# A recurrent attention with two expert layers on one core: later copies of the inverses, two sets of inversion buffers, one subtract on VectorE, and another order of the beginning

## The chip, the cores and the metric

The kernel runs on one core of a Trainium2 chip. The metric is device time in microseconds (us) of one execution. The engines are named as the profile does: PE is TensorE (its weight loads are PEld), DVE is VectorE, ACT is ScalarE, POOL is GpSimd, SP is SyncE. A row with SPq or ACTq is the issue of a DMA by SyncE's or ScalarE's queue.

## What is computed

The inputs are 4 batches of 8 heads with 768 steps of width 40, and the weights of two token layers. Cut to what matters:

```python
for t in range(S):                       # 768 steps, state 40x40 per head
    y[:, :, t] = einsum('bhd,bhde->bhe', rt, state)
    Sa = einsum('bhde,bhe->bhd', state, at)
    state = state * wt - Sa x bt + vt x kt          # outer products
x = y as 3072 tokens of width 320
x = ((x @ w_a) * (x @ w_b)) @ w_out                 # 320 -> 1536 -> 320
out = sum over 4 experts e of p_e * (relu(x @ w1[e]) @ w2[e])   # 320 -> 1024 -> 320
```

## The kernel before

The recurrence is turned into chunks of 32 steps. There are N = 48 chunks, numbered n: 24 in time for each of NPASS = 2 halves of the batch, so chunk n needs the state that chunk n-2 left. SUP = 4 chunks share one inversion; I call four chunks n = 4s to 4s+3 a superstep, s = n // 4.

What is done for one chunk n, by its functions:

- `fetch(n)` loads e1 (decay factors, k, b and a; 419 KB). `decay(n)` is the scan R on VectorE (L131), `inverse(n)` a reciprocal (L139) and a small copy lc, `scale(n)` makes ke (L150) and a part of A (L153). `prep_T(n)` multiplies these on TensorE (L171, L175); VectorE masks a part into A (L178), ScalarE copies a part to tbs (L180) and the rest to L (L183).
- After `prep_T` of the last chunk of a superstep, `invert(s)` takes the four chunks' triangular blocks: ScalarE's queue writes tbs to DRAM as td (L191), SyncE's queue reads it back rearranged as tblk (L196) and fills X, called xblk in rows, from a constant (L198); then 31 pairs of small steps, a product tmp (L204) and a subtract from xblk (L207). The first inversion runs on VectorE, the others on POOL. `place(s)` writes xblk to DRAM as xd (L216), reads it back as xr (L219), and ScalarE copies xr to xs (L222, two copies).
- `load(n)` brings e2 (L229) and v (into G, L232). `rhs(n)` (L298) makes rh, `u(n)` (L318) multiplies it with the inverse xs, `sy(n)` (L341) gives the output ys and the state; `cf`, `q` and `tr` are small products that ride in the same PSUM banks.
- When four chunks are done, `mo.load` sends ys through DRAM (xt, L507) and reads it as xf (L511, L513); `mo.split` makes its high and low parts xh and xl (L413, L414).

The first token layer, Moe1, is a stream of matmuls that is fed into the loop over chunks in small portions, so that TensorE has work while the chunk's own steps wait for other engines. A block of it is 16 matmuls `l1` (L554) into a PSUM tile, then a (copy, ScalarE, L556), g (product, VectorE, L558), gh (ScalarE, L413), gl = g - gh (POOL, L414, in `parts_of`), and 8 matmuls `l2` (L586 to L594). `moe(k)` lets k matmuls of the stream through; the stream stops at `ready`, the number of token tiles that have been split. Its weights come in a packed form and are converted once, in the beginning, on VectorE (L487 to L491), ScalarE and POOL (L500), in steps that `fill` and `ensure` pull. The second token layer, Moe2, follows after the loop.

The order on every engine is the order of the program text, as long as the loop over chunks runs: engines take their instructions in that order and wait for what they need. The loop's body before, from the function `body`:

```python
at.rhs(n, "B", n + 1); load(n + 2)
... at.inverse(n + LEAD); at.scale(n + LEAD, v)      # LEAD = 7
moe(g[0]); at.u(n, "B", n + 1)
if cc == 3: steps(100); at.place(s + 1)
if cc == 0: mo.split(s - 1); ready += 1
moe(g[1]); at.sy(n, ys, "B", n + 2)
if cc == 3: mo.load(s, ys)
at.prep_T(m)                                          # m = n + LEAD
if m % 4 == 3: inv = at.invert(m // 4, pool); steps(2)
fetch(m + 1); at.decay(m + 1); moe(g[2])
```

Here cc = n % 4. `steps(k)` and, after every third matmul of the stream, `moe` advance the inversion by one instruction.

## Time and profile before

| | before |
|---|---|
| median of 3 runs | 1903.65 us (1900.16 to 1903.71) |
| the profiled execution | 1898.02 us, its span 1896.2 us |
| mean granted TensorE clock | 0.895 |
| PE busy | 1500.1 us (79%) |
| DVE busy | 764.5 us (40%) |
| ACT busy | 598.4 us (32%) |
| POOL busy | 524.2 us (28%) |

Busy shares are means over stages with different limits. The page's view in 40 slices shows TensorE busy four to eight tenths up to about 1100 us (beginning and loop) and nine tenths or more from there on (rest of Moe1, and Moe2), and a granted clock of about eight tenths in the first part. The granted clock is a mean of two levels, 1.2 GHz (0.5 in the rows) and 2.4 GHz (1.0). A wait in a row is idle time of the engine ahead of that instruction, with the one that ended it behind an arrow.

### The profile page before, as it was taken

The page shows a single profiled execution, that of the slowest core. Times are in us where ns is not written, and L with a number is a line of the kernel's source. Part 1 is how long each engine was busy: PE and PEld are TensorE (multiplying, and loading weights), DVE is VectorE, ACT ScalarE, POOL GpSimd, SP SyncE. Part 2 cuts the span into 40 slices and gives each one's busy share as a digit, 9 for nine tenths or more (in the row PEclk, how much of TensorE's full clock was granted, in tenths as well). Part 3 has the DMA queues.
Part 4 walks back from the last instruction along what each step waited for, and adds up shares of the span by engine and source line. Part 5 has one row for each costly group of instructions (what it writes and reads, how often), then busy time and mean ns, then how long its engine had stood idle before and what let it go on. Part 6 is the DMA issues. An engine that isn't in the chain of part 4 may idle for free.

```text
span 1896.2 us, 40330 instructions
## 1 busy us (share of the span) xinstructions
PE 1500.1 (79%) x17202; PEld 1352.3 (71%) x17202; DVE 764.5 (40%) x1451; ACT 598.4 (32%) x1454; POOL 524.2 (28%) x976
## 2 busy tenths in 40 slices
PE   4341476777777776858686899999999999999998
PEld 3331465767667676757586799877789999999997
DVE  5667543434434342525343223544532222232222
ACT  3232232333332332323233235666521121121111
POOL 5157352434434251616253425100100020010000
PEclk9855687878888888879798999999999999999999
DMA  7350213222223132232222214755720010000000
GB/s 200 94 189 12 53 38 86 60 72 51 76 46 79 44 78 49 77 73 56 70 60 67 49 56 132 209 147 146 234 86 1 1 62 1 1 1 15 15 29 30
DMA packets 141741, 134.76 MB, mean 71 GB/s; under 512 B 94576, under 2 KB 111600, under 8 KB 141552
## 3 DMA queue, kind: packets, MB, share of 16 engines
q1 hardware_dynamic: 116448, 128.72, 25.2%
q10 hardware_dynamic: 25104, 3.37, 1.2%
q8 instruction: 137, 2.24, 0.5%
q14 instruction: 52, 0.43, 0.1%
HBM read 113.97 MB, written 18.09 MB: 70 GB/s over the span
## 4 chain that ended last, share of the span: by engine, by line


## 5 line engine op out<-in xcount | busy, mean ns | idle before, releaser
L554 PE MATMUL l<-xh,w 128*128 128x256 f32 x1440 | 351.0, 325 | 192.4 <-DVE g L558 170.5
L554 PEld LDWEIGHTS l<-xh,w 128*128 128x128 f32 x1440 | 269.4, 220 | 206.5 <-DVE g L558 176.5
L554 PE MATMUL l<-xl,w 128*128 128x256 f32 x864 | 269.0, 317 | 5.8 <-POOL xl L414 4.6
L685 DVE SCALAR_TENSOR_TENSOR hl<-l,hh 128x512 fp32r<-128x512 f32 x192 | 132.3, 690 | 343.6 <-ACT hh L684 343.5
L698 PE MATMUL o<-h,hh 128*128 128x320 f32 x768 | 239.0, 311 | 7.4 <-ACT hh L684 5.2
L700 PE MATMUL o<-h,hl 128*128 128x320 f32 x768 | 239.6, 313 | 4.6 <-DVE hl L685 4.2
L684 ACT ACTIVATE hh<-l 128x512 fp32r<-128x512 f32 x192 | 114.0, 594 | 395.5 <-PE l L681 395.5
L699 PE MATMUL o<-l,hh 128*128 128x320 f32 x768 | 236.9, 309 | 0.0
L554 PEld LDWEIGHTS l<-xl,w 128*128 128x128 f32 x864 | 191.3, 221 | 11.5 <-POOL xl L414 10.4
L414 POOL TENSOR_TENSOR gl<-g,gh 128x256 fp32r<-128x256 f32 x144 | 105.7, 734 | 338.6 <-ACT gh L413 338.6
L204 POOL TENSOR_TENSOR tmp<-tblk,xblk 128x126 f32<-128x126 f32 (+22 forms) x341 | 143.0, 419 | 198.4 <-DMA xblk<-cst 155.5
L414 POOL TENSOR_TENSOR l<-r,h 128x512 fp32r<-128x512 f32 (+1 forms) x32 | 46.5, 1477 | 494.0 <-ACT h L413 494.0
L698 PEld LDWEIGHTS o<-h,hh 128*128 128x128 f32 x768 | 144.2, 188 | 23.7 <-ACT hh L684 13.1
L700 PEld LDWEIGHTS o<-h,hl 128*128 128x128 f32 x768 | 144.0, 188 | 11.6 <-DVE hl L685 11.6
L681 PE MATMUL l<-XL,h 128*128 128x512 f32 x384 | 151.7, 395 | 0.0
L681 PE MATMUL l<-XH,h 128*128 128x512 f32 x384 | 151.6, 395 | 0.0
L558 DVE TENSOR_TENSOR g<-l,a 128x256 f32<-128x256 f32 x144 | 60.6, 421 | 223.2 <-ACT a L556 204.6
L681 PE MATMUL l<-XH,l 128*128 128x512 f32 x384 | 149.9, 390 | 0.0
L699 PEld LDWEIGHTS o<-l,hh 128*128 128x128 f32 x768 | 144.2, 188 | 6.7
L413 ACT CAST gh<-g 128x256 fp32r<-128x256 f32 x144 | 58.4, 405 | 275.0 <-DVE g L558 274.8
L207 POOL TENSOR_TENSOR xblk<-xblk,tmp 128x126 f32<-128x126 f32 (+22 forms) x341 | 131.7, 386 | 20.6
L586 PE MATMUL o<-gh,wo 128*128 128x256 f32 x288 | 83.5, 290 | 48.6 <-ACT gh L413 48.1
(121 smaller groups left out, 2617.9 us busy)
## 6 DMA issues: line engine op xcount, KB each, us to landing
g<-e SPq DMA_DIRECT2D x48, 419.2 KB
e<-e SPq DMA_DIRECT2D x46, 419.2 KB
e<-e SPq DMA_DIRECT2D x48, 208.0 KB
wr<-wab SPq DMA_DIRECT2D x12, 512.0 KB
tblk<-td SPq DMA_DIRECT2D x24, 256.0 KB
r<-w SPq DMA_DIRECT2D x8, 768.0 KB
gx<-wab SPq DMA_DIRECT2D x12, 512.0 KB
r<-w SPq DMA_DIRECT2D x8, 640.0 KB
```

Source lines behind the costliest of these rows:

```text
L204: eng.tensor_tensor(out=t, in0=tb[:, k + 1:, k:k + 1].to_broadcast([128, m, c]), in1=X[:, k:k + 1, :c].to_broadcast([128, m, c]), op=ALU.mult)
L207: eng.tensor_tensor(out=X[:, k + 1:, :c], in0=X[:, k + 1:, :c], in1=t, op=ALU.subtract)
L414: eng.tensor_tensor(out=lo, in0=raw, in1=hi, op=ALU.subtract)
L554: nc.tensor.matmul(o, l, r, start=j == 0, stop=j == len(ops) - 1)
L558: nc.vector.tensor_tensor(out=g[:], in0=ps[:, 256:512], in1=a[:], op=ALU.mult)
L586: nc.tensor.matmul(o, h, gh[:], start=s and f == 0, stop=False)
L681: nc.tensor.matmul(ps[:], l, r, start=i == 0, stop=i == len(ops) - 1)
L684: nc.scalar.activation(hh[:], ps[:], AF.Relu)
L685: nc.vector.scalar_tensor_tensor(out=hl[:], in0=ps[:], scalar=0.0, in1=hh[:], op0=ALU.max, op1=ALU.subtract)
L698: nc.tensor.matmul(o[:], hh[:, s], h2[:, k], start=first, stop=False)
L699: nc.tensor.matmul(o[:], hh[:, s], lo2[:, k], start=False, stop=False)
L700: nc.tensor.matmul(o[:], hl[:, s], h2[:, k], start=False, stop=last)
```

## The change

1. `place` no longer copies xr to xs. A new function `settle(s)` does, and the loop calls it in the next superstep, directly ahead of u of its first chunk. `both` runs two chunks' steps in turn.
2. tblk and xx get two buffers each, by s % 2; e1 gets one instead of two (tag e1, bufs=1).
3. gl is made by VectorE, six matmuls of the stream after gh (`high`, `low`); xl too.
4. In the loop, the load of e2 and v and the fetch of e1 for chunk m + 1 stand behind `scale(m)` at the top of an iteration; `decay(m + 1)` stays at its end. The portions are 20, 28, 24 instead of 24, 24, 24 (18, 26, 22 instead of 15, 17, 18 for chunks 5 to 7), and the inversion advances after every second matmul.
5. The beginning is reordered: prep of chunks 0 to 7 first, the second inversion directly behind the first one's place and spread over the steps of chunks 0 to 3, the conversion of weights taken in smaller parts and for the most part after chunk 4. The unit blocks in L come by DMA from a longer constant instead of a memset and copies (`ones`), and the weights are loaded by ScalarE's queue.

```diff
-E1 = ("e1", "e1", "ys", 0, 1, "tblk", "ys", "e1")
+E1 = ("e1", "ys", "tblk1", 0, 1, "e1", "ys", "e1")
...
     def ones(self, h):
-        nc.gpsimd.memset(self.L[0][32:64, h], 0.0)
-        for P in range(2):
-            r = slice(SROW[P], SROW[P] + 40)
-            nc.scalar.copy(self.L[P][r, h].rearrange("p i a d -> p (i a) d"), self.idn[r].unsqueeze(1).to_broadcast([40, SUP * 8, 40]))
+        for P, r in enumerate((slice(0, 64), slice(64, 104))):
+            m = r.stop - r.start
+            self.nc.sync.dma_start(self.L[P][r, SUP * h:SUP * h + SUP].rearrange("p i a d -> p i (a d)"),
+                                   self.unit[r].unsqueeze(1).to_broadcast([m, SUP, 320]))
...
-            e1 = self.pool.tile([104, 1032], F32, tag=tag, name=f"e1_{n}", bufs=2 if tag == "e1" else 1)[:]
+            e1 = self.pool.tile([104, 1032], F32, tag=tag, name=f"e1_{n}", bufs=1)[:]
...
-        tb = pool.tile([128, 32, 32], F32, tag="tblk", name=f"tblk_{s}", bufs=1)
+        tb = pool.tile([128, 32, 32], F32, tag=f"tblk{s % 2}", name=f"tblk_{s}", bufs=1)
...
-        xr = pool.tile([128, 2, SUP * 4, 16], F32, tag="xx", name=f"xr_{s}", bufs=1)
+        xr = pool.tile([128, 2, SUP * 4, 16], F32, tag=f"xx{s % 2}", name=f"xr_{s}", bufs=1)
         for z in range(2):
             nc.sync.dma_start(xr[:, z], xd[z].rearrange("a p c -> p a c"))
+        self.sup[s] = xr
+
+    def settle(self, s):
+        nc, pool, xr = self.nc, self.pool, self.sup[s]
         xs = pool.tile([128, SUP * 4, 16, 2], F32, tag="xs", name=f"xs_{s}", bufs=1)
         for z in range(2):
             nc.scalar.copy(xs[:, :, :, z], xr[:, z])
...
-            self.nc.sync.dma_start(raw[:], src[:, m * at:m * at + m])
+            self.nc.scalar.dma_start(raw[:], src[:, m * at:m * at + m])
...
-            split(nc, xf[:, f], xh[:, f], xl[:, f], nc.gpsimd)
+            split(nc, xf[:, f], xh[:, f], xl[:, f], nc.vector)
...
-        self.later.append([8, lambda: self.parts_of(t, i, g)])
+        self.later.append([8, lambda: self.high(t, i, g)])
...
+        self.nc.scalar.copy(gh[:], g[:])
+        self.later.append([6, lambda: self.low(t, i, g, gh)])
...
-        split(self.nc, g[:], gh[:], gl[:], self.nc.gpsimd)
+        self.nc.vector.tensor_tensor(out=gl[:], in0=g[:], in1=gh[:], op=ALU.subtract)
...
+        at.prep_T(7, "B")
+        inv0, inv = inv, at.invert(1, pool)
+        steps(1)
+        whole(inv0)
+        at.place(0)
+        steps(1)
...
+            g = (18, 26, 22) if n < RING else (20, 28, 24)
             at.rhs(n, "B", n + 1)
-            load(n + 2)
+            if n + 2 < N:
+                if n > SUP + 1:
+                    at.loade(n + 2)
+                if n > SUP:
+                    at.loadv(n + 2)
...
+            elif m < N:
+                at.inverse(m)
+                at.scale(m, v)
+                fetch(m + 1)
             moe(g[0])
...
+            if cc == 0:
+                at.settle(s)
             at.u(n, "B", n + 1)
...
-                    inv, every = at.invert(m // SUP, pool), 3
+                    inv, every = at.invert(m // SUP, pool), 2
                     steps(2)
-            fetch(m + 1)
```

What the change moves in the loop, by the programs' own order of instructions. SyncE's queue from place in iteration 19 to the inversion's loads in iteration 20, before (e1_27 and e1_28 are the chunks' e1; xt and xf are the trip of ys to the token layer):

```order
L216 DMA xd_5_6016<-xblk_5_5252 64x512 x2
L219 DMA xr_5_6019<-xd_5_6016 128x16x16 x2
L507 DMA xt_4_6097<-ys_16_5173 40x4x256 x2
L511 DMA xf_4_6100<-xt_4_6097 128x2x256
L513 DMA xf_4_6100<-xt_4_6097 64x256 x2
L125 DMA e1_27_6137<-e1 104x1032
L229 DMA e2_22_6203<-e2 104x512
L232 DMA G0_1_102<-vt 32x4x104
L232 DMA G1_1_105<-vt 32x4x104
L196 DMA tblk_6_6404<-td_6_6401 64x1024 x2
L198 DMA xblk_6_6407<-cst 128x512
L125 DMA e1_28_6409<-e1 104x1032
```

The same place after, which begins with e1_27, at the top of iteration 19:

```order
L124 DMA e1_27_5964<-e1 104x1032
L215 DMA xd_5_6034<-xblk_5_5274 64x512 x2
L218 DMA xr_5_6037<-xd_5_6034 128x16x16 x2
L516 DMA xt_4_6116<-ys_16_5195 40x4x256 x2
L520 DMA xf_4_6119<-xt_4_6116 128x2x256
L522 DMA xf_4_6119<-xt_4_6116 64x256 x2
L231 DMA e2_22_6220<-e2 104x512
L238 DMA G0_1_102<-vt 32x4x104
L238 DMA G1_1_105<-vt 32x4x104
L124 DMA e1_28_6232<-e1 104x1032
L195 DMA tblk_6_6426<-td_6_6423 64x1024 x2
L197 DMA xblk_6_6429<-cst 128x512
```

Each e1 has moved ahead of the waits for xd, xt and td that stood before it. ScalarE in iteration 19, from u on, before (psU is u's PSUM tile, xs_5 the inverse for chunks 20 to 23):

```order
L322 ACTIVATE G0_1_102<-psU_19_5977 32x2x4x40
L322 ACTIVATE G1_1_105<-psU_19_5977 32x2x4x40
L272 COPY G0_2_103<-psU_19_5977 40x2x4x32
L272 COPY G1_2_106<-psU_19_5977 40x2x4x32
L222 COPY xs_5_6022<-xr_5_6019 128x256 x2
L556 COPY a_3_8_6028<-l1_3_8_5959 128x256
L413 CAST gh_3_8_6039<-g_3_8_6030 128x256
L180 COPY tbs_6_5520<-psT_26_6104 32x256 x2
```

ScalarE after, from the rhs of chunk 20 to its u:

```order
L308 COPY rh_20_6216<-psR_20_6191 128x288
L293 COPY S_21_6218<-psR_20_6191 104x320
L140 COPY lc_27_6226<-R_27_6156 104x8
L565 COPY a_3_11_6248<-l1_3_11_6186 128x256
L572 CAST gh_3_11_6259<-g_3_11_6250 128x256
L225 COPY xs_5_6262<-xr_5_6037 128x256 x2
L328 ACTIVATE G0_2_103<-psU_20_6265 32x2x4x40
L328 ACTIVATE G1_2_106<-psU_20_6265 32x2x4x40
```

The copies xs_5 have moved from behind u of chunk 19, ahead of a and gh of a block, to just ahead of u of chunk 20. POOL at the beginning of the inversion for chunks 20 to 23, before:

```order
L204 TENSOR_TENSOR tmp_5_0_5260<-tblk_5_5249,xblk_5_5252 128x31
L207 TENSOR_TENSOR xblk_5_5252<-xblk_5_5252,tmp_5_0_5260 128x31
L204 TENSOR_TENSOR tmp_5_1_5273<-tblk_5_5249,xblk_5_5252 128x30
L414 TENSOR_TENSOR gl_3_0_5278<-g_3_0_5265,gh_3_0_5277 128x256
L207 TENSOR_TENSOR xblk_5_5252<-xblk_5_5252,tmp_5_1_5273 128x30
L204 TENSOR_TENSOR tmp_5_2_5287<-tblk_5_5249,xblk_5_5252 128x58
```

The same place after, with the steps alone:

```order
L203 TENSOR_TENSOR tmp_5_0_5282<-tblk_5_5271,xblk_5_5274 128x31
L206 TENSOR_TENSOR xblk_5_5274<-xblk_5_5274,tmp_5_0_5282 128x31
L203 TENSOR_TENSOR tmp_5_1_5289<-tblk_5_5271,xblk_5_5274 128x30
L206 TENSOR_TENSOR xblk_5_5274<-xblk_5_5274,tmp_5_1_5289 128x30
L203 TENSOR_TENSOR tmp_5_2_5296<-tblk_5_5271,xblk_5_5274 128x58
L206 TENSOR_TENSOR xblk_5_5274<-xblk_5_5274,tmp_5_2_5296 128x29x2
```

gl no longer stands between the steps; on POOL there is nothing else in the loop's later part.

## Rows read from the trace of the kernel before

**Rows 1.** Busy time by stretch: start:end us, length, us busy (x count), clock, DMA, GB/s

```profile
core 0: us, PE busy (x) PEld busy (x) DVE busy (x) ACT busy (x) POOL busy (x), PEclk, DMA share, GB/s
...
230.40:284.50 54.10, 39.54 (x765) 36.11 (x766) 26.25 (x50) 18.10 (x54) 29.47 (x68) 0.78 0.19 41
284.50:1002.10 717.60, 523.51 (x8962) 477.89 (x8961) 299.45 (x586) 227.72 (x664) 281.84 (x615) 0.84 0.28 66
```

**Rows 2.** The same view for iterations 17 to 20; one row, and their sum

```profile
515.21:530.21 15.00, 14.24 (x283) 13.24 (x282) 9.51 (x19) 6.43 (x21) 12.83 (x27) 1.00 0.09 23
...
sum 89.25, PE 65.43 PEld 59.98 DVE 37.28 ACT 28.49 POOL 35.10; mean PE 16.36 PEld 15.00 DVE 9.32 ACT 7.12 POOL 8.77
```

**Rows 3.** Waits of TensorE, 284.5 to 1002.1 us: who for whom, total us, times, longest

```profile
PE l L554 <- DVE g L558: 163.1, 24, 11.0
PE l L554 <- ACT xh L413: 17.8, 8, 6.9
```

**Rows 4.** Timeline, end of iteration 16: start us, us, engine, line, what [idle before, releaser]

```profile
485.93 0.31 ACTq L191 DMA_DIRECT2D td<-tbs  x1
...
490.98 0.38 SPq L125 DMA_DIRECT2D e<-e  x1
...
495.20 0.25 POOL L204 TENSOR_TENSOR tmp<-tblk,xblk 128x31 f32<-128x31 f32 x1 [16.17 <-DMA xblk<-cst]
...
497.18 0.71 DVE L131 TENSOR_TENSOR_SCAN R<-e,acst 104x264 f32<-104x264 f32 x1 [11.36 <-DMA e<-e]
...
498.26 0.58 PE L554 MATMUL l<-xh,w 128*128 128x256 f32 x1 [9.44 <-DVE g L558]
```

**Rows 5.** Timeline, iteration 19

```profile
536.03 1.13 SPq L216 DMA_DIRECT2D xd<-xblk  x2
...
544.37 0.42 ACT L222 COPY xs<-xr 128x256 f32<-128x256 f32 x1 [1.08 <-DMA xr<-xd]
...
545.77 0.58 PE L554 MATMUL l<-xh,w 128*128 128x256 f32 x1 [4.78 <-DVE g L558]
```

**Rows 6.** Timeline of VectorE, end of iteration 19

```profile
556.74 0.71 DVE L131 TENSOR_TENSOR_SCAN R<-e,acst 104x264 f32<-104x264 f32 x1 [7.19 <-DMA e<-e]
```

**Rows 7.** Timeline of TensorE, iteration 20

```profile
562.00 0.70 PE L268 MATMUL psU<-e,S 40*40 40x32 f32 x32
...
565.80 0.51 PE L554 MATMUL l<-xh,w 128*128 128x256 f32 x1 [1.61 <-ACT xh L413]
```

**Rows 8.** Timeline of TensorE, iteration 41

```profile
1030.49 0.58 PE L590 MATMUL o<-gl,wo 128*128 128x256 f32 x1 [5.74 <-POOL gl L414]
```

**Rows 9.** VectorE by line, 284.5 to 1002.1 us: count, busy us, mean ns, idle before

```profile
L558 DVE TENSOR_TENSOR g<-l,a 128x256 f32<-128x256 f32 x96 | 40.3, 420 | 135.8 <-ACT a L556 125.8 <-POOL tmp L204 8.9
```

**Rows 10.** Timeline of ScalarE, iteration 18

```profile
519.17 0.87 ACT L322 ACTIVATE G<-psU 32x320 f32<-32x320 f32 x2
...
527.38 0.36 ACT L180 COPY tbs<-psT 32x256 f32<-32x256 f32 x1 [0.48 <-DVE A L178]
```

**Rows 11.** POOL by line, 284.5 to 1002.1 us

```profile
L204 POOL TENSOR_TENSOR tmp<-tblk,xblk 128x126 f32<-128x126 f32 (+22 forms) x248 | 105.8, 426 | 155.5 <-DMA xblk<-cst 118.9 <-DMA e<-e 17.8
L207 POOL TENSOR_TENSOR xblk<-xblk,tmp 128x126 f32<-128x126 f32 (+22 forms) x248 | 94.2, 380 | 14.4
L414 POOL TENSOR_TENSOR gl<-g,gh 128x256 fp32r<-128x256 f32 x95 | 69.7, 734 | 232.4 <-ACT gh L413 232.4
```

**Rows 12.** Timeline, beginning: TensorE's u of chunk 0 and 4, POOL's second inversion

```profile
71.26 2.14 PE L318 MATMUL psU<-rh,xs 32*32 32x72 f32 x64 [21.28 <-ACT xs L222]
...
98.70 0.25 POOL L204 TENSOR_TENSOR tmp<-tblk,xblk 128x31 f32<-128x31 f32 x1 [0.30 <-DMA xblk<-cst]
...
176.82 0.29 POOL L207 TENSOR_TENSOR xblk<-xblk,tmp 128x16 f32<-128x16 f32 x1
...
205.38 1.18 PE L318 MATMUL psU<-rh,xs 32*32 32x72 f32 x32
```

**Rows 13.** Busy time in the stretch in which TensorE stood, columns of rows 1

```profile
153.50:201.58 48.08, 0.00 (x0) 0.00 (x0) 37.14 (x54) 12.68 (x29) 39.03 (x60) 0.53 0.08 11
```

## What I predict

> **What bounds the kernel now.** I read the profile by stages first. The profiled execution took 1898.02 us; the median of the three timed runs is 1903.65 us, 5.6 us higher, and I make the sum against the profiled execution and move the result up by that. I call four consecutive iterations of the main loop, n = 4s to 4s+3, a superstep, since one inversion serves four chunks. Chunks 8 to 39 take 284.5 to 1002.1 us, 717.6 us or 89.7 us per superstep, with TensorE busy 523.5 us and a mean granted clock of 0.84 [rows 1]. One iteration in that stretch shows what the work itself needs: 515.21 to 530.21 us, 15.00 us, TensorE busy 14.24 us at clock 1.00, while the four iterations of which it is one need 89.25 us [rows 2]. So 32 iterations are worth 456 us of TensorE at full clock; of the other 262 us, 194 are idle and about 68 are the same work at the half clock (523.5 - 456).
>
> The idle time has named ends. In that stretch TensorE waited 163.1 us for g (VectorE) in 24 places, three per superstep, and 17.8 us for xh in 8 places [rows 3]. The three per superstep are these. (a) 9.4 us at 498.26: VectorE sat 11.4 us before a scan R that waited for its e1 chunk, and g stands behind R; that e1 transfer was issued by SyncE behind tblk, which waits for td (485.93 on ScalarE's queue) [rows 4]. (b) 4.8 us at 545.77: ScalarE, which must make a before VectorE can make g, sat in the two copies xs until xr had landed [rows 5]. (c) The scan at 556.74 waited 7.2 us for e1, this time behind the xt/xf round trip [rows 6]. A fourth, small one is xh: 1.6 us at 565.80 [rows 7]. Part of the work after such gaps runs at the lower of the two clock levels (1.2 instead of 2.4 GHz): that is the 68 us.
>
> **The change part by part.**
>
> *Order of SyncE, single e1 buffer.* e1 for the next chunk is now issued at the top of an iteration, right behind the scale that frees the one buffer, in front of place, xt/xf and tblk; its scan comes at the end of the same iteration. That removes (a) and (c). The new wait: SyncE stands until scale is over, about 5 us into the iteration; the transfer needs at most 6.2 us in the worst case shown (issue 490.98, scan 497.18 [rows 4]), and the scan comes some 14 us after the iteration's start. Margin 3 us; I take a cost of nothing, and 6 us per superstep if the margin is gone (first rival).
>
> *xs copies.* settle puts them in the next superstep, behind g of the blocks that are already due and directly ahead of u. That removes (b). What is late next is xr itself, through the inversion's chain, which I sum below.
>
> *gl on VectorE, POOL left with the inversion.* Chunk 41 shows what gl on POOL costs when (a) is not there: 5.7 us of TensorE waiting for gl [rows 8], since gl stands behind the first instruction of the inversion, which waits for xblk. Removing (a) alone would bring that wait out in each superstep; so I count gl's move as what lets (a) go, not as a gain of its own. Its price is 12 VectorE subtracts per superstep; the nearest row is g, 0.42 us [rows 9], so 5 us in a superstep in which VectorE is busy 37.3 of 89.25 us, and 9.5 of 15.0 in the undisturbed iteration [rows 2]: hidden, 0 to 5 us, I take 0.
>
> A row speaks against it: in the same stretch g waited 8.9 us for POOL's tmp [rows 9]. The Trainium skill (SBUF — State Buffer, "SBUF: two separate sides") says that VectorE instructions with two SBUF inputs and GpSimd instructions hold one port pair in turn, each for its whole length. By that rule each of the 15 subtracts (12 gl, 3 xl) would also hold up the inversion. The second rival prices this from rows.
>
> *The chain of one inversion.* It now decides whether u has to wait. From u to the last copy of tbs 8.6 us (519.17 to 527.74) [rows 10], 0.5 us more for four more matmuls ahead of sy, 3.2 us for the wait on xh (below); td to POOL's first step 9.3 us [rows 4]; 62 POOL instructions of 0.426 and 0.380 us, 25.0 us [rows 11], and some 5 us between them, 30 us; end of the inversion to the end of xs 8.8 us (536.03 to 544.79) [rows 5]; u itself 1.7 us. Sum 62.1 us. Before, the same chain had 41 us instead of 30 in it (495.20 to 536.03), since gl stood among the POOL steps.
>
> *TensorE in a superstep.* 4 x 14.24 = 57.0 us, some 1.2 us of short waits in sy (0.76 us per iteration so far [rows 2], with four more matmuls ahead of sy to cover it), and the wait on xh. That wait grows: the budgets 20, 28, 24 use up exactly the matmuls that exist when u of a new superstep comes, so TensorE stands from the end of u (562.70) to 565.80, 3.1 to 3.2 us instead of 1.6 [rows 7]; if xf is late by the time SyncE spends on place, 1.5 us more. Half clock after it: 0 to 2.5 us, taken as 1. Sum 62.5 to 65 us. Chain and TensorE come out nearly equal; I take 64 us per superstep, bounds 60 (four undisturbed iterations) and 67. Eight supersteps: 512 instead of 717.6, **-205.6 us** (-182 to -238).
>
> *Chunks 40 to 47.* The gl wait of 5.7 us [rows 8] and one of kind (b), 4.8 us [rows 5], go, with some 2 us of half clock; the two waits on xh grow by 1.6 us each, at most by 4: **-9 us** (-4 to -14).
>
> *The beginning.* The first u hardly moves. Before it came at 71.26 us [rows 12]. The transfers that replace ScalarE's copies let td go some 4 us earlier, but two more prep_T and a prep (4 us) now stand in the inversion's way; I take 0. The second inversion gains: before it ran on POOL from 98.70 to 177.04 us, mixed with the conversion of the weights, while TensorE stood for 48.1 us (153.50 to 201.58); u of chunk 4 came at 205.38 [rows 12, 13]. Now its tblk is queued directly behind xr of the first one, so POOL can start at about 75 us; 30 us of its own and the subtracts of two and a half blocks (in that gap POOL spent 39.0 us on 7 blocks and the last 14 steps of the inversion, so 3.5 to 4 us per block), 9 us: over at 114, xs at 123, u of chunk 4 at about 124 instead of 205. But the conversion isn't gone. In the gap VectorE was busy 37.1 us for 7 blocks, 5.1 us each counting its last work [rows 13], and 9.4 blocks are still open at chunk 4: 48 us. With four iterations of VectorE at 26.25/3 = 8.8 us [rows 1], two preps that come later than before (8 us) and 11 gl (5 us), that is 96 us; at a busy share of 0.77 (the gap) to 1, 125 to 96 us. Chunk 8 then begins at 220 to 250 us, I take 240: **-44.5 us** (-35 to -65). The weight transfers move to ScalarE's queue, where they may wait for the second inversion's own transfers; until 124 us nothing else is due there.
>
> *After the loop.* By the budgets 324 instead of 339 matmuls are left, 15 at no more than 0.2 us (72 of them lie in the 15.00 us of [rows 2], beside others): **-2 us**. The second layer has none of the changed instructions.
>
> Sum: -205.6 - 9 - 44.5 - 2 = -261 us; 1898 - 261 = 1637, on the scale of the median **1642 us**.
>
> **The rivals.**
>
> 1. *A stall is moved, not removed*: e1 lands after its scan, or xr after u. For it: both margins are about 3 us, and SyncE stands in place until POOL is through, with xt, xf, e2 and e1 behind it. Against it: e1 is issued 9 us ahead of its scan. Price: one gap of 6 us and 2 us of half clock per superstep, 72 us: 1642 + 64 = 1706.
> 2. *VectorE and POOL hold each other up.* For it: [rows 9]. Against it: gl itself leaves POOL with 8.8 us per superstep (12 x 0.73 [rows 11]). Price: 15 subtracts, each holding POOL up by 0.42 us, 6 us on the chain of 62.1: 68 to 70 per superstep, 1642 + 44 = 1686. This is also the time by the rule cited above.
> 3. *The other side, slower*: the inversion on POOL becomes the bound. u waits for xs, so every us of POOL beyond 32 goes onto the superstep. Slower than before from a superstep of 96 us on (717.6 + 55.5 over 8), that is when 62 POOL steps need 64 us instead of 30, 1.03 us each. For it: POOL meets 15 more VectorE instructions with two SBUF inputs. At two and a half times today's 0.48 us: 74 us, 106 per superstep, 1642 + 336 = 1978. Against it: where the two engines met so far, g lost 8.9 us in all over eight supersteps [rows 9].
> 4. *Better than forecast*: chain and wait on xh overlap, no half clock, 60 us per superstep and the larger gain at the beginning: 1642 - 32 - 20 = 1590.
>
> **How the numbers follow.** Forecast 0.55, rival 1 0.15, rival 2 0.17, rival 3 0.03, rival 4 0.10. The predicted time is the forecast's, 1642. The range leaves out rival 3, the far end of rival 4 and of rival 1 (a gap at two places): low end 1898 - 238 - 65 - 14 - 2 + 5.6 = 1585; high end rival 1 with the smaller gain at the beginning, 1706 + 10 = 1716, taken as 1720. A measurement of this kernel can tell about 0.2%, 4 us, from no change. Faster by more than that: all but rival 3 and a little for what I don't see, 0.95; within 0.02; slower 0.03.
>
> **What would show it.** Right: no VectorE scan that waits several us for e1; no ScalarE copy xs that waits for xr between chunks 8 and 39; TensorE's waits there near 50 us instead of 194, ended by xh; POOL's inversion over 30 us after its first step; chunk 8 at about 240 us, and VectorE the busiest engine between chunks 4 and 8. Wrong: a wait of u for xs in each superstep (chain too long), scans that still wait for e1, or POOL steps of 0.5 us and more next to gl on VectorE.

## The result, and the profile after

The changed kernel takes 1728.43 us (median of four runs, 1727.24 to 1729.1) against 1903.68 us (1900.16 to 1907.55): a ratio of 0.908, 95% interval 0.906 to 0.910. It is faster by 175 us; 261 had been forecast, and the time lies 8 us above the range. The profiled execution took 1729.1 us, its span is 1727.3.

By stages, as [rows 1] and [rows 2] of before (stretch in us, its length, busy time and count of each engine, granted TensorE clock, DMA share, GB/s); the first three rows end where rh of chunks 8, 40 and 47 starts and the fourth at the end of the span, the fifth is chunks 4 to 7, the last two are iterations n = 20 and 21:

```profile
0.00:273.50 273.50, 128.97 (x2273) 118.18 (x2273) 177.11 (x335) 79.38 (x223) 122.52 (x203) 0.78 0.42 107
273.50:836.10 562.60, 484.05 (x8961) 447.06 (x8961) 346.67 (x703) 226.98 (x664) 206.65 (x496) 0.93 0.34 82
836.10:945.00 108.90, 93.74 (x1672) 86.80 (x1671) 46.18 (x109) 39.65 (x107) 23.81 (x62) 0.92 0.21 51
945.00:1727.30 782.30, 756.86 (x4302) 674.51 (x4302) 267.67 (x486) 247.18 (x459) 53.28 (x33) 0.99 0.24 70
152.90:273.50 120.60, 75.58 (x1159) 70.09 (x1159) 91.79 (x166) 45.60 (x124) 59.07 (x99) 0.69 0.24 59
483.90:507.50 23.60, 16.62 (x283) 15.16 (x281) 11.19 (x25) 8.93 (x27) 0.00 (x0) 0.86 0.25 61
507.50:523.10 15.60, 14.20 (x279) 13.09 (x280) 10.72 (x22) 6.45 (x20) 7.13 (x19) 1.00 0.56 144
```

| stage | before | after | difference | forecast |
|---|---|---|---|---|
| up to chunk 8 | 284.5 | 273.5 | -11.0 | -44.5 |
| chunks 8 to 39 | 717.6 | 562.6 | -155.0 | -205.6 |
| chunks 40 to 46 | 113.2 | 108.9 | -4.3 | -9 |
| from chunk 47 on | 780.9 | 782.3 | +1.4 | -2 |

The forecast's last two numbers were made for chunks 40 to 47 and for what follows them.

So the loop gained three quarters of what was forecast (70.3 us per superstep, not 64), the beginning a quarter. Who TensorE waited for in chunks 8 to 39 (engine, matmul, whom it waited for: us in all, times, longest), as [rows 3]:

```profile
PE l L563 <- ACT xh L422: 24.7, 8, 3.1
PE psU L324 <- ACT xs L225: 23.6, 8, 3.3
PE psY L347 <- ACT G L278: 20.3, 22, 1.3
PE o L599 <- ACT x L612: 6.8, 8, 0.9
PE psY L253 <- DMA e<-e: 3.2, 5, 1.1
```

The 163 us for g are gone. Two waits per superstep stand out: xh, which was forecast (3.1 us), and xs ahead of u, which was not; the prediction had named it as a sign of being wrong, with the inversion's chain as its reason. ScalarE in that iteration (start, us, engine, line; in brackets the idle time ahead and who ended it), then VectorE, SyncE's queue and POOL around it:

```profile
484.57 0.38 ACT L565 COPY a<-l 128x256 f32<-128x256 f32 x1
487.29 0.40 ACT L572 CAST gh<-g 128x256 fp32r<-128x256 f32 x1 [2.34 <-DVE g L567]
487.60 0.72 ACT L225 COPY xs<-xr 128x256 f32<-128x256 f32 x2
489.58 0.87 ACT L328 ACTIVATE G<-psU 32x320 f32<-32x320 f32 x2 [1.26 <-PE psU L274]
491.37 0.75 ACT L278 COPY G<-psU 40x256 f32<-40x256 f32 x2 [0.93 <-DVE G L330]
492.14 1.02 ACT L422 CAST xh<-xf 128x256 fp32r<-128x256 f32 x3
```

```profile
483.42 1.74 DVE L138 RECIPROCAL gam<-R 104x256 f32<-104x256 f32 x1
485.08 0.63 DVE L149 TENSOR_TENSOR ke<-e,R 104x512 f32<-104x512 f32 x1
485.62 0.84 DVE L152 TENSOR_TENSOR A<-e,gam 40x256 f32<-40x256 f32 x2
486.50 0.42 DVE L577 TENSOR_TENSOR gl<-g,gh 128x256 fp32r<-128x256 f32 x1
486.84 0.42 DVE L567 TENSOR_TENSOR g<-l,a 128x256 f32<-128x256 f32 x1
```

```profile
474.56 1.13 SPq L215 DMA_DIRECT2D xd<-xblk  x2
477.67 2.45 SPq L218 DMA_DIRECT2D xr<-xd  x2
```

```profile
443.82 0.25 POOL L203 TENSOR_TENSOR tmp<-tblk,xblk 128x31 f32<-128x31 f32 x1 [39.91 <-DMA xblk<-cst]
...
474.31 0.22 POOL L206 TENSOR_TENSOR xblk<-xblk,tmp 128x16 f32<-128x16 f32 x1
```

xs starts without any idle time of its own, over seven us after the second transfer of xr was issued. So it did not wait for late data (settle_up, below, bears that out): it stood in ScalarE's queue behind gh, gh waited 2.34 us for g, and g stood behind reciprocal, ke, A and gl on VectorE. The inversion itself took 30.7 us (443.82 to 474.53), as forecast.

In the beginning ScalarE is held up too, in front of transfers that it issues itself. ScalarE's queue, with the transfers it issues (ACTq), around rh of chunk 0 and of chunk 4; then TensorE, then one row of VectorE, then POOL in the second inversion:

```profile
74.34 0.44 ACTq L453 DMA_DIRECT2D wr<-wab  x1
81.25 0.35 ACTq L453 DMA_DIRECT2D wor<-wo  x1
81.64 0.70 ACT L308 COPY rh<-psR 128x288 f32<-128x288 f32 x2 [13.61 <-DMA xr<-xd]
89.91 0.62 ACT L506 CAST w<-cvA 128x512 fp32r<-128x512 f32 x1 [7.57 <-DVE cvA L500]
90.44 0.72 ACT L225 COPY xs<-xr 128x256 f32<-128x256 f32 x2
...
139.79 0.39 ACTq L453 DMA_DIRECT2D wr<-wab  x1
146.79 0.34 ACTq L453 DMA_DIRECT2D wor<-wo  x1
...
152.86 0.40 ACT L308 COPY rh<-psR 128x288 f32<-128x288 f32 x1 [14.49 <-issue]
```

```profile
86.41 0.66 PE L253 MATMUL psC<-e 40*32 40x32 f32 x32 [13.47 <-DMA e<-e]
91.21 2.14 PE L324 MATMUL psU<-rh,xs 32*32 32x72 f32 x64 [4.15 <-ACT xs L225]
...
153.41 2.27 PE L170 MATMUL psT<-A,ke 40*64 40x32 f32 x32 [12.10 <-DVE A L152]
...
164.00 1.18 PE L324 MATMUL psU<-rh,xs 32*32 32x72 f32 x32 [7.73 <-ACT xs L225]
```

```profile
87.12 0.85 DVE L257 TENSOR_TENSOR G<-psC,acst 32x256 f32<-32x256 f32 x2 [15.55 <-PE psC L253]
```

```profile
102.55 1.52 POOL L509 TENSOR_TENSOR w<-cvA,cvH 64x256 fp32r<-64x256 f32 x2 [6.76 <-ACT cvH L506]
109.01 1.01 POOL L509 TENSOR_TENSOR wo<-cvA,wo 128x256 fp32r<-128x256 f32 x2 [4.94 <-ACT wo L506]
```

Between 139.79 and 152.8 us ScalarE does nothing but issue these transfers and stand in front of them; rh of chunk 4, whose matmuls ended at 136.6, and xs behind it stand in the same queue. The trace names xr as the end of the first wait (81.64) and nothing for the second ("issue"). That the issues wait for earlier transfers (those of xr and e1 on SyncE's queue are under way then) is inferred, not shown.

u of chunk 0 waits for more than its rh, which was done at 82.3. cf(2) (the row of 86.41) waits 13.47 us for e2, VectorE's G waits for cf(2), the conversion stands behind that G on VectorE, ScalarE's w waits 7.57 us for the conversion, and xs, without idle time of its own, stands behind w. So xs is late for the same kind of reason as in the loop, with another instruction in front of it.

### The profile page after: what moved, and what is told of

The parts are those of the page before. It is cut to its first block, busy times and chain, and to the rows that moved or that the text cites. A ratio compares the mean times of both kernels' runs of the same rounds, so it can differ in the third digit from the quotient of the medians.

```text
span 1727.3 us, 40183 instructions
## 1 busy us (share of the span) xinstructions
PE 1463.6 (85%) x17202; PEld 1326.5 (77%) x17202; DVE 837.6 (48%) x1631; ACT 593.2 (34%) x1450; POOL 406.3 (24%) x794
## 3 DMA queue, kind: packets, MB, share of 16 engines
q1 hardware_dynamic: 113012, 117.99, 25.8%
## 4 chain that ended last, share of the span: by engine, by line
## 5 line engine op out<-in xcount | busy, mean ns | idle before, releaser
L563 PE MATMUL l<-xh,w 128*128 128x256 f32 x1440 | 316.5, 303 | 34.1 <-ACT xh L422 33.0
L563 PEld LDWEIGHTS l<-xh,w 128*128 128x128 f32 x1440 | 255.2, 208 | 37.8 <-ACT xh L422 34.5
L563 PE MATMUL l<-xl,w 128*128 128x256 f32 x864 | 263.7, 311 | 0.1
L203 POOL TENSOR_TENSOR tmp<-tblk,xblk 128x126 f32<-128x126 f32 (+22 forms) x341 | 139.0, 408 | 424.3 <-DMA xblk<-cst 320.5
L563 PEld LDWEIGHTS l<-xl,w 128*128 128x128 f32 x864 | 179.5, 208 | 6.2 <-DVE xl L423 2.1
L206 POOL TENSOR_TENSOR xblk<-xblk,tmp 128x126 f32<-128x126 f32 (+22 forms) x341 | 145.9, 428 | 26.9 <-POOL tmp L203 0.2
L170 PE MATMUL psT<-A,ke 40*64 40x32 f32 x1536 | 67.0, 240 | 64.1 <-DVE A L152 28.4
L170 PEld LDWEIGHTS psT<-A,ke 40*64 40x64 f32 x1536 | 60.7, 158 | 67.9 <-issue 36.2
L179 ACT COPY tbs<-psT 32x256 f32<-32x256 f32 x96 | 35.0, 365 | 219.5 <-DVE A L177 217.1
```

The costliest lines, as they stand in the source:

```text
L170: nc.tensor.matmul(T[P][KROW[P]:KROW[P] + 64, a], ke[r, a].rearrange("p y t -> p (y t)"), self.A[P][r, k, a], start=True, stop=True)
L203: eng.tensor_tensor(out=t, in0=tb[:, k + 1:, k:k + 1].to_broadcast([128, m, c]), in1=X[:, k:k + 1, :c].to_broadcast([128, m, c]), op=ALU.mult)
L206: eng.tensor_tensor(out=X[:, k + 1:, :c], in0=X[:, k + 1:, :c], in1=t, op=ALU.subtract)
L563: nc.tensor.matmul(o, l, r, start=j == 0, stop=j == len(ops) - 1)
```

## The experiments

Each kernel is the changed one with the edits named. The table gives the median, the ratio to the kernel before with its 95% interval, the start of chunk 8 and the mean superstep in chunks 8 to 39, both read from the starts of the copies rh.

| kernel | median us | ratio | chunk 8 at | superstep us |
|---|---|---|---|---|
| before | 1903.7 | 1 | 284.5 | 89.7 |
| changed | 1728.4 | 0.906-0.910 | 273.5 | 70.3 |
| settle_up | 1708.6 | 0.896-0.899 | 269.7 | 68.3 |
| short_inv | 1720.1 | 0.902-0.905 | 272.7 | 70.2 |
| split_up | 1690.3 | 0.886-0.889 | 274.3 | 66.6 |
| both_up | 1678.6 | 0.880-0.885 | 269.5 | 65.7 |
| undo_e1 | 1876.7 | 0.983-0.988 | 275.6 | 88.3 |
| gl_pool | 1830.3 | 0.957-0.965 | 275.8 | 80.9 |
| undo_settle | 1781.1 | 0.932-0.935 | 282.3 | 75.3 |
| beg_weights | 1725.4 | 0.904-0.909 | 269.3 | 70.0 |
| beg_all | 1710.2 | 0.896-0.900 | 255.7 | 70.3 |
| no_conv | 1705.2 | 0.894-0.899 | 248.3 | 69.9 |
| best1 | 1674.5 | 0.877-0.880 | 256.9 | 66.1 |
| best2 | 1673.2 | 0.876-0.879 | 257.9 | 66.2 |
| best1_inv_first | 1677.3 | 0.879-0.882 | 259.6 | 65.6 |
| best3 | 1672.3 | 0.878-0.884 | 255.4 | 66.3 |
| best4 | 1651.2 | 0.864-0.871 | 251.4 | 63.9 |

### What u waits for in the loop

```diff
 at.rhs(n, "B", n + 1)
+if cc == 0: at.settle(s)          # settle_up
 ...
 moe(g[0])
-if cc == 0: at.settle(s)          # settle_up
+if cc == 0 and s > 1: mo.split(s - 1)   # split_up
 at.u(n, "B", n + 1)
-if cc == 0 and s > 1: mo.split(s - 1)   # split_up
```

> The changed kernel with one edit: the two copies xs (settle) stand directly behind rhs at the head of the iteration, ahead of the first matmuls of the first layer, instead of directly ahead of u. The changed kernel has, at each of the ten supersteps of the loop, a 3.3 us gap before u(4s) that ends with xs, and runs at the half clock behind it. Theory A (order on ScalarE): xr has long landed, and xs waits in ScalarE's queue behind gh, which waits for g behind VectorE's reciprocal and scale; then the 3.3 us gap goes, and some of the half clock with it: 4 to 5 us per superstep, 1728 - 40 = 1688 us (1680 to 1700). Rival B (the chain of the inversion through POOL, xd and xr is too long): xs now blocks ScalarE earlier until xr lands, the gap stays or grows: 1728 or slower.

> The changed kernel with 21 instead of 31 steps in each inversion from the third on, so the last ten steps of every block inverse are left out; xs is ready some 6 us sooner. Theory A (order on ScalarE): nothing in the loop waits for the inversion, the 3.3 us gap before u(4s) stays: 1728 us within 4 (1720 at most if POOL's shorter stay also lets xt and xf go earlier). Rival B (chain too long): the gap goes, 1728 - 10 x 4 = 1688 us. Rival C (VectorE and POOL hold each other up): VectorE instructions get shorter with less POOL beside them, 1 us or more per superstep, 1715 or lower.

short_inv has `range(31 if s < 2 else 21)` in the inversion's loop. In settle_up xs starts 0.6 us behind rh instead of 3.75, again without idle time (475.10, second row), so xr is there even then, 4.6 us behind the issue of its second transfer, and the gap ahead of u is gone; xh is now what is late:

```profile
474.49 0.39 ACT L308 COPY rh<-psR 128x288 f32<-128x288 f32 x1
...
475.10 0.75 ACT L225 COPY xs<-xr 128x256 f32<-128x256 f32 x2
...
480.91 1.02 ACT L422 CAST xh<-xf 128x256 fp32r<-128x256 f32 x3
```

The waits of TensorE in seven supersteps (chunks 12 to 39), settle_up first, short_inv second:

```profile
PE l L563 <- ACT xh L422: 29.5, 7, 4.3
```

```profile
PE psU L324 <- ACT xs L225: 22.9, 7, 3.3
```

With ten steps less in each inversion the wait for xs is the same as in the changed kernel, which has 22.9 us in these seven supersteps too. So theory A holds in the steady loop and the chain of the inversion does not decide there. It does at the very end: at chunk 44, where iterations are only 12 to 13 us long, the gap ahead of u fell from 4.9 to 1.1 us in short_inv. (The median is 8 us lower; the span of the profiled execution is 5.7 us shorter, and 3.7 of it lie in chunks 40 to 46.) Rival C, by which VectorE would gain 1 us or more per superstep, is refuted in the loop too: the superstep is 70.2 instead of 70.3 us. settle_up gained 20 us, half of what I expected: u comes earlier and the wait for xh grew by some 1.1 us per superstep, and TensorE's busy time, which holds the half clock, fell only from 60.5 to 60.1 us per superstep.

> The changed kernel with one edit: split (copies xh on ScalarE, xl on VectorE) stands behind the copies xs and ahead of u instead of behind u. The changed kernel has a second gap of 3.1 us behind u(4s), since the matmuls of the first layer wait for xh, which ScalarE makes behind the copies out of u. Theory: xf has landed by then, xh is made while u runs, and the gap behind u goes: 3 us per superstep, 1728 - 25 to 30 = about 1700 us, with less half clock perhaps 1695. Rival: xf lands only about then, xh holds up ScalarE and with it the copies out of u, and the gap moves to sy: within 10 us of 1728.

> Both edits: xs behind rhs at the head of the iteration, and split ahead of u. If both gaps have the named causes, no gap above 1.5 us is left in the steady loop, the clock there stays near 1.0 and a superstep takes about 62 us instead of 70.3: 1728 - 10 x 7.5 = 1653 us (1645 to 1670). If one of the causes is wrong, one gap stays and the time is 1680 to 1700.

split_up gained 38 us, 3.7 us per superstep, more than expected: no wait for xh is left in its list, and the wait for xs is as before. Both together gained 50, less than forecast: one gap of 1.7 us stays behind u, in which xh stands behind gh and gh behind VectorE's scale.

### What each part of the change is worth

```diff
-fetch(m + 1)                      # undo_e1: no longer behind scale
+fetch(m + 1); at.decay(m + 1)     # undo_e1: ahead of the scan again
-self.nc.vector.tensor_tensor(out=gl[:], ...)    # gl_pool
+self.nc.gpsimd.tensor_tensor(out=gl[:], ...)    # gl_pool
 at.place(s + 1)
+at.settle(s + 1)                  # undo_settle
-if cc == 0: at.settle(s)          # undo_settle: now only for s = 1
```

> The changed kernel with the order of SyncE undone: the next e1 is fetched directly ahead of its scan at the end of the iteration again (one buffer, as in the changed kernel), behind place, xt/xf, e2, vt and tblk. This measures what that part of the change is worth. By the rows of the kernel before (waits (a) 9.4 us and (c) 7.2 us per superstep, and half clock behind them) 15 to 20 us per superstep come back: 1728 + 10 x 17 = 1900 us (1860 to 1910). Rival: with gl off POOL and the xs copies elsewhere, VectorE's scan no longer holds up g so long, and only some 5 us per superstep come back: 1780.

> The changed kernel with gl on POOL again instead of VectorE, in the same place of the order. By chunk 41 of the kernel before, gl then stands behind the first instruction of the inversion, which waits for xblk: 5.7 us of TensorE per superstep, and the 62 steps share POOL with 12 gl of 0.7 us: 1728 + 10 x 6 to 8 = 1795 us (1780 to 1830). Rival (VectorE and POOL hold each other up, so that gl on VectorE costs as much as it saves): 1728 within 15.

> The changed kernel with the copies xs back where they were before, directly behind place (so ScalarE stands in them until xr has landed, and what a and gh need stands behind them), for all supersteps from the third on. This measures what the move of xs alone is worth. By the rows of the kernel before 4.8 us of g per superstep come back, with some 2 us of half clock, and the 3.3 us gap ahead of u that the changed kernel has goes: 3 to 4 us per superstep net, 1728 + 35 = 1763 us (1745 to 1790). Rival: the two waits weigh the same, within 8 us of 1728.

In seven supersteps (the first row is VectorE of undo_e1, the second TensorE of gl_pool, the third ScalarE of undo_settle):

```profile
DVE R L130 <- DMA e<-e: 133.1, 14, 13.0
```

```profile
PE o L603 <- POOL gl L577: 61.8, 18, 7.0
```

```profile
ACT xs L225 <- DMA xr<-xd: 48.7, 14, 7.3
```

Each wait that the prediction had named comes back on its engine: the scan for e1 (the superstep is 18.0 us longer; 17 expected), gl on POOL (10.6; 6 to 8 expected), xs for xr (5.0; 3 to 4 expected). The times are 1876.7, 1830.3 (at the end of what was expected) and 1781.1 us. undo_e1 keeps the single e1 buffer, where the kernel before had two, so it is no pure return to the old order; TensorE there waits 79.9 us for x, the copies out of the second product, and 35.7 for gl, and not for g as before. The three add up to 33.6 us per superstep where the whole change gained 19.4, so the worth of one part depends on the others. That the waits partly hide each other would explain it, but other parts of the change may cost something too; this was not taken apart. That VectorE and POOL hold each other up so much that gl on VectorE costs what it saves is refuted: gl_pool is 102 us slower than the changed kernel.

### The beginning

```diff
-mo.fetch(2)  # beg_weights: behind place(0); now behind sy(0), sy(1); fetch(4) behind sy(2), sy(3)
-for i in range(8, mo.NK1, 2): mo.fetch(i)
+# fetch(6), (8), (10) behind u(4), sy(4), u(5)
-whole(at.cf(2))   # beg_all: ahead of u(0); now behind sy(0), sy(1)
-at.place(1); prep(8, v); at.prep_T(8); fetch(9)
+prep(8, v); fetch(9); at.place(1); at.prep_T(8)   # beg_all
```

> The changed kernel with one edit: the transfers of the first layer's weights stay on ScalarE's queue but are issued later (those of fetch(2) behind the first sy, fetch(4) behind the second, fetch(6), (8), (10) behind u(4), sy(4), u(5)). In the changed kernel ScalarE stands twice in front of such an issue: rh of chunk 0 starts at 81.6 us though its matmuls end at 73, and from 138.4 to 152.9 us it does nothing else, while rh of chunk 4 waits. Theory (ScalarE stands in the issues, which wait for transfers of SyncE): rh of chunk 4 comes at about 138 instead of 152.9 us, xs of chunk 4 at 150 instead of 163.2, and chunk 8 starts 10 to 15 us earlier than 273.5: 1728 - 12 = 1716 us (1708 to 1722). Rival 1 (VectorE, which does the conversion, sets the beginning): chunk 8 starts at 273 as before, 1728 within 4. Rival 2 (later weights hold up the conversion): slower than 1732.

> The same edit, and two more: cf(2) stands behind the first sy instead of ahead of u(0) (in the changed kernel TensorE waits 13.5 us there for e2 of chunk 2, up to 86.4 us, with u(0) behind it), and the e1 of chunk 9 is issued ahead of place(1) instead of behind it (TensorE waits 12.1 us for A of chunk 9, up to 153.4). Theory: u(0) moves from 91.2 to about 82 us and the stretch up to chunk 8 shortens by 20 to 25 us in all: 1728 - 22 = 1706 us (1698 to 1714). Rival (VectorE's conversion sets the beginning): the first chunks come earlier, chunk 8 doesn't: 1728 within 5.

In beg_weights rh of chunks 0 and 4 (ScalarE) start 9.8 and 19.1 us earlier, without an issue in front:

```profile
71.88 0.40 ACT L308 COPY rh<-psR 128x288 f32<-128x288 f32 x1 [4.01 <-PE psR L304]
...
133.79 0.40 ACT L308 COPY rh<-psR 128x288 f32<-128x288 f32 x1
```

But chunk 8 came only 4.2 us earlier (10 to 15 expected), and the time, 1725.4 us, is not told apart from the changed kernel's (1723.3 to 1728.8 against 1727.2 to 1729.1). u of chunk 0 came 4.8 us earlier (86.40), just as the end of cf(2)'s wait for e2 did (81.62 instead of 86.41). u of chunk 4 came 9.1 us earlier (154.89), with TensorE still waiting for A of chunk 9 (7.6 us; its e1 is fetched behind xr) and for xs (7.7 us); the way from there to chunk 8 then took 4.9 us more, and why was not taken apart. With the two further edits u of chunk 0 comes at 78.25, u of chunk 4 at 140.25, and chunk 8 starts 17.8 us earlier (20 to 25 expected; the time, 1710.2, lies in the expected range). So ScalarE's issues were one of three things in a row, and taking away this one alone brought little; the others were not tried alone.

> best1 with all 62 steps of the second inversion queued on POOL ahead of the subtracts of the weights' conversion, instead of mixed with them. In the changed kernel that inversion takes 49.3 us (85.7 to 135.0) where the prediction had 39, and POOL stands 6.8 and 4.9 us of it in subtracts that wait for ScalarE. Theory: the inversion takes about 28 us, xs of chunk 4 is ready earlier, and chunk 8 starts 6 to 10 us earlier than in best1. Rival (by then VectorE's conversion and the e1 transfers set the beginning): chunk 8 within 3 us of best1, or later, since VectorE runs out of buffers for the conversion.

> The changed kernel with two of the three VectorE instructions that convert a piece of the first layer's weights left out (the low bits and the sign are left out, so the output is another). It tells what sets chunks 4 to 7, which take 120.6 us (152.9 to 273.5) in the changed kernel. Theory (VectorE's conversion sets them): some 9 blocks of the conversion lie there, at 2.5 pieces of 1.0 to 1.4 us less each some 25 to 30 us of VectorE; the stretch falls to 95 us or less, chunk 8 starts at 248 or earlier. Rival (the chain of e1, scan, scale with its one buffer, or POOL, sets them): the stretch stays at 115 us or more.

```diff
 fill(4); steps(12)  ->  steps(100); fill(4)                  # best1_inv_first
-v.scalar_tensor_tensor(out=A, in0=hw, scalar=0xC0000000, ...) # no_conv
-v.scalar_tensor_tensor(out=A, in0=lw, scalar=29, ...)         # no_conv
```

With all steps queued first, the second inversion took 29.2 us from its first subtract (80.65 to 109.83) instead of 42.2 in best1, but chunk 8 came 2.7 us later (6 to 10 earlier expected). As the rival had it, VectorE now waits in the conversion for POOL's subtract to be done with a buffer, which it does not in best1:

```profile
DVE cvA L496 <- POOL w L509: 7.8, 1, 7.8
```

no_conv shortened chunks 4 to 7 from 120.6 to 98.9 us. VectorE's conversion is on the path there, with 22 us of the 25 to 30 expected; the stretch did not fall to the 95 us of the theory, and what remains of it was not taken apart.

### All edits together

> The four edits that each made the changed kernel faster, together: xs at the head of the iteration, split ahead of u, the weights' transfers issued later, cf(2) and the e1 of chunk 9 moved. If they add up (1678.6 with the first two, 18.3 us for the other two) 1660 us (1652 to 1668).

> The same, and at the first iteration of each superstep the reciprocal and scale of VectorE (and the fetch behind them) stand behind the first 20 matmuls of the first layer instead of ahead of them. With the first two edits alone 1.7 us of TensorE per superstep were left behind u, where xh stands on ScalarE behind gh, gh waits 1.7 us for g, and g stands behind VectorE's 3 us of reciprocal and scale. Theory (order on VectorE): that gap goes with some half clock, 2 to 3 us per superstep: 1660 - 25 = 1637 us (1630 to 1648). Rival (xf has only just landed by then): 1660 within 5.

> best1 with another order in the stream of the first layer: where a new block of tokens begins, the eight matmuls of the second product that stand next (which need nothing of the new block) go ahead of the first eight-matmul groups that need xh. So TensorE has eight matmuls to do behind u while ScalarE makes xh and the copies out of u. In best1 1.7 us of TensorE are idle there per superstep and the clock falls behind them (18.9 to 21 us for that iteration instead of 15 to 15.5). Theory: the gap goes and the clock stays up: 3 to 4 us per superstep, 1674.5 - 32 = 1642 us (1635 to 1655). Rival (the gap moves to the next wait, xl or a): 1665 or more.

> best3 with (18, 26, 19) instead of (18, 26, 22) matmuls of the first layer per iteration in chunks 4 to 7. In best3 the eight matmuls moved ahead were all issued before u (its 20 at the head of the iteration reach to them, 454.97 to 456.12 us), so that nothing was left behind u and the gap stayed (2.1 us, ended by xh). With twelve fewer in the first four chunks, eight are left when u of a new superstep comes. Theory (TensorE only lacks work that needs nothing of xh): the gap falls to 1 us or less and the clock stays up, 3 us per superstep, 1673 - 30 = 1643 us (1635 to 1658). Rival (what comes next, a and xl, ends no earlier): 1665 or more.

best1 missed its 1660 by 14 us: the start of chunk 8 improved by 12.6 us against both_up, but 3.2 us were lost again in the loop and 3.9 in chunks 40 to 46, where single iterations ran longer at a lower clock. best2 was no gain: xh then waits for xf, which has just landed, and xl behind the scale. In best3 the eight matmuls still went ahead of u. best4 is best3 with a lag of twelve matmuls:

```diff
 # Moe1.run, best3: where a new block of tokens begins
 if i1 == 0:
+    yield from self.l2(t, i)
     yield t1
+    yield from self.l1(t1, i1)
+    continue
 # body, best4
-g = (18, 26, 22) if n < RING else (20, 28, 24)
+g = (18, 26, 19) if n < RING else (20, 28, 24)
```

Two stretches of best4, chunks 8 to 39 and chunks 12 to 15 alone; then TensorE's wait for xh in seven supersteps:

```profile
251.40:762.60 511.20, 470.60 (x8971) 429.91 (x8972) 348.34 (x705) 226.29 (x665) 205.23 (x496) 0.99 0.38 91
314.90:377.70 62.80, 58.06 (x1122) 53.12 (x1121) 43.62 (x89) 28.08 (x84) 25.58 (x62) 1.00 0.39 92
```

```profile
PE l L566 <- ACT xh L422: 3.2, 4, 1.0
```

The gap is gone, the clock is 0.99, and a superstep takes 63.9 us, the length that had been forecast for the changed kernel. best4 beats both kernels: 1651.2 us, 0.868 of the time before (0.864 to 0.871). The lag of twelve matmuls was not tried without best3's order, so whether both are needed stays open.

## Why the prediction was wrong, point by point

- **The order of SyncE and gl: right.** No scan waits for e1 in the steady loop, iterations n = 4s+1 to 4s+3 take 15.0 to 15.8 us (two of the 24 take 16.6), nearly as the undisturbed one of [rows 2], and undo_e1 and gl_pool bring back what [rows 4], [rows 6] and [rows 8] had shown.
- **The xs copies: the step that failed in the loop.** "What is late next is xr itself, through the inversion's chain". The inversion took the 30 us of the sum, but xr was not late. I put the copies "behind g of the blocks that are already due" and gave that no price: I summed when the data would be there, and not how long what stands ahead of xs in ScalarE's queue would take, gh of a block that waits for g, behind 3.2 us of VectorE's reciprocal and scale at the head of the iteration. The wait is 23.6 us in eight supersteps, 3.0 each. settle_up and short_inv show it. The sign "a wait of u for xs in each superstep" came, and its reason, "chain too long", did not hold.
- **TensorE in a superstep: mis-sized terms.** The forecast was 57.0 of work, 1.2 of short waits, 3.1 for xh, 1 of half clock, and the upper half of 62.5 to 65. Measured: 60.5 us busy (484.05 / 8), of which 58.1 are the work at clock 1.00 (best4, chunks 12 to 15) and 2.4 the half clock; xh 3.1 as forecast; short waits 3.8 (20.3 + 6.8 + 3.2 over 8); xs 3.0. Together 70.4, 8.1 above the 62.3 to which the forecast's own terms add up: xs makes 3.0 of it, the short waits 2.6, the half clock 1.4, the work 1.1. Of the short waits the largest is that of sy for ScalarE's G (2.5 us per superstep; 1.1 in the kernel before); why it grew was not tried. Two gaps instead of one do not explain the half clock: with one of them gone TensorE's busy time is still 60.1 us (settle_up, 480.91 / 8) and 59.8 us (split_up, 478.79 / 8). Why it is more than 1 us stays open.
- **Chunks 40 to 46: within the bounds** (-4.3 for -4 to -14). There the chain of the inversion does bind, at chunk 44. What follows came out at +1.4 instead of -2: with the 15 matmuls less TensorE was busy 2.3 us less, but it stood 3.6 us longer, which was not taken apart.
- **The beginning: the step that failed most.** "The first u hardly moves": u(0) came at 91.21, not 71.26 as in [rows 12], since xs stood behind w in ScalarE's queue, w waited for VectorE's conversion, and VectorE for cf(2), whose e2 stands behind place and tblk on SyncE. That rh stood behind the weights' issues came on top, but did not decide here: with rh 9.8 us earlier and cf(2) in its place u(0) came only 4.8 us earlier (beg_weights). Of the weights' transfers the prediction said "they may wait for the second inversion's own transfers; until 124 us nothing else is due there": they did wait, and rh of chunk 0, rh of chunk 4 and xs were due there. The second inversion started at 85.71 instead of 75, took 49 us instead of 39, because its steps stood behind subtracts that waited for ScalarE (6.76 and 4.94 us), and xs was done 29 us behind its end instead of 9. So u of chunk 4 came at 164.00 instead of 124; of these 40 us, the parts were 10.7 at the inversion's start (4.8 of them went when the weights were issued later, in beg_weights), 10 in its length, 20 behind it. From there to chunk 8 the forecast was 116 us and the time 109.5; that VectorE's conversion is on the path of this stretch was right (no_conv). beg_all brought 17.8 of the missing 33.5 us back; the other 15.7 were not taken apart.
- **The rivals.** Rival 1 (a stall is moved, not removed) is nearest in kind: xr was there, but xs was not, and the price was 3 us and half clock per superstep instead of 8. (Its price is given as 72 us and summed as 64.) Rival 2 gave a superstep of 68 to 70 us, and so by luck nearly the measured 70.3, for a wrong reason: the 62 steps of an inversion were busy 25.8 us (0.41 and 0.43 us each) instead of 25.0, 0.8 us more where the rival had 6. The Trainium skill (SBUF — State Buffer, "SBUF: two separate sides") says that a VectorE instruction with two SBUF inputs and a GpSimd instruction that reads SBUF block each other, the later one for the whole length of the earlier. The trace agrees, with one such pair of rows at the end of this document.
- **The range** missed by 8 us. The loop gained 27 us less than the least of its own bounds (-155.0 for -182), the beginning 24 us less (-11 for -35). By its stages' own bounds the sum would have ended at about 1681 us; rival 1 had moved the upper end to 1720, which left room for one of these two misses and not for both.

## What to carry to other kernels

When an instruction is moved to just ahead of its use on an engine that works in order, read what stands in front of it there and what that waits for, not only when its data land. A transfer issued from a compute engine's queue can wait like any other instruction, and everything behind it waits too (rh of chunk 4 behind 13 us of issues, here): put it where nothing is due. Fill a wait of TensorE with matmuls that need nothing of what is awaited, since the gaps here cost their own length and mostly some half clock behind it.

## What the runs showed of the hardware

Issuing a transfer cost ScalarE 0.33 to 0.45 us where nothing held it up, with up to 6.6 us of standing ahead of one where something did (140.18 to 146.79). The Trainium skill (DMA: Bandwidth & Descriptors, "Issuing engines are not separate DMA queues") says that issuing from several engines only saves the sequencer's time to initiate a DMA, which is usually small beside the DMA itself. The 0.33 to 0.45 us are that time here. The standing comes on top of it, and it was what held up rh.

In both_up an iteration with a gap of 1.7 us behind u had a mean granted clock of 0.91 (463.3 to 482.3), and in best4, with waits of 1.3 us and less, chunks 12 to 15 had 1.00. That is no rule: in best1 an iteration whose longest gap was 1.2 us ran at 0.81 (470.8 to 489.0), and what tells the two apart stays open.

A subtract of POOL with two SBUF inputs held up VectorE: the same conversion instruction took 0.49 us with POOL idle and 1.54 us beside one that had begun 0.07 us before it (VectorE twice, then POOL, in the changed kernel; `cvA` of `wor` is 128x320 each time):

```profile
154.63 0.49 DVE L500 SCALAR_TENSOR_TENSOR cvA<-wor,cvA 128x320 uint32<-128x320 uint32 x1
...
158.55 1.54 DVE L500 SCALAR_TENSOR_TENSOR cvA<-wor,cvA 128x320 uint32<-128x320 uint32 x1
```

```profile
158.48 1.26 POOL L509 TENSOR_TENSOR w<-cvA,w 128x512 fp32r<-128x512 f32 x1 [1.28 <-ACT w L506]
```
